# A linear-attention and two-layer expert kernel on one core: the weight slices 5 to 7 are used by the first two token chunks in turn

## The chip, the cores and the metric

One Trainium2 chip; the kernel runs on one of its cores. The engines spoken of are PE (TensorE, matmuls), DVE (VectorE), ACT (ScalarE), POOL (GpSimd) and the queue of SP (SyncE), from which nearly all transfers are issued. The metric is the device time of one execution in microseconds (us); smaller is better.

## What is computed

The reference, cut to what matters. The stages that the change touches are the attention and the first three products of the first expert block (`a`, `b`, `h`).

```python
# attention, per batch (4) and head (8), seq 576, head_dim 64
q_s = softmax(q, axis=-1)                  # over the 64 columns of a row
k_s = softmax(k, axis=2)                   # over the 576 positions
x   = q_s @ (k_s.T @ v)                    # -> 2304 tokens x 512
# first block: w1, w2 512 x 1024, w3 1024 x 1024, w_out 1024 x 512 (given in 8 bytes an element)
a = x @ w1; b = x @ w2
x = (a * b @ w3) @ w_out                   # -> 2304 x 512
# second block: four experts, each relu(x @ e1) @ e2, weighted by domain_probs
```

## The kernel before

Tokens are columns. The 2304 tokens are cut into chunks of 512 (the last one 256); chunk 0 lies in batch 0 (576 tokens a batch), chunk 1 needs the last 64 tokens of batch 0 and 448 of batch 1. The first block's feature dimension is cut into NF = 8 slices f of 128.

**Work per slice.** `ab_step(c, f)` makes `a` and `b` of chunk c for slice f: two accumulations of 12 matmuls of 512 columns (three per 128 rows, since each operand is held as a high and a low part), then a copy of `a` by ACT (L566) and the product with `b` by DVE (L567). With an even f, or any chunk but 0, its two PSUM banks come from `ps_w`, which has two; chunk 0 with odd f takes the banks of `ps_y`. `unit(u)` multiplies a part of w3 with w_out, 12 matmuls; W = w3 @ w_out takes the place of w3 and w_out later.

**Weights come in 8 bytes an element and are converted on the core.** A job is a pair of them: job f is slice f of w1 and w2, job 8 + u is w_out and w3 for unit u, later jobs are two parts of w3. `load_to` issues the transfers (four raw buffers, so job n + 4 waits for job n), `b_to` issues ACT's L140, DVE's four operations L144, L147, L151, L155 and the split into high part (ACT L103) and low part (DVE L104). `convert(n)` issues the loads up to job n + 3 and the conversions up to job n - 1.

**Order.** Work is issued in numbered slots; a scheduler then fixes the order on each engine, early issues first, as far as their inputs are ready by its own estimate. At run time each engine takes its instructions in that fixed order. Slots 6 to 13 (AB0) hold `ab_step(0, 0)` to `ab_step(0, 7)`; slots 14 to 21 (AB1) hold `ab_step(1, 7)` down to `ab_step(1, 0)`, each followed by a unit; slots 22 to 29 (W1) the other eight units; 30 on the product with W. Slices 0 to 5 are written to DRAM during AB0 (`save_w12`) and read again during AB1 (`load_w12`); slices 6 and 7 are kept in SBUF for chunk 1. Weight slices, x, products and W share a pool of 28 tiles.

**Batch 1** must be ready as x before slot 14. `K_SLOT[1]` and `Q_SLOT[1]` give the slots of its four head pairs' keys (6, 7, 8, 9) and its two query halves (6, 8): `k_max`, one slot later `k_exp`, then `k_v` (PE and DVE, ACT), `q_exp`, `q_norm` and `q_turn` (transposes), and `x_stage`, at most in the slot before `X_SLOT[1]`. Loads go three slots earlier. The small PSUM results of these steps share the two banks of `ps_a`. Query half (1, 1) is in `ON_SCALAR`: its exponential is 18 activations of 64 columns with the maximum as bias and a running sum, in place of a subtraction and a sum of the whole tile by DVE. `hold` with `AFTER_JOB` puts an instruction behind the last conversion of a job, but only if that job has been issued by then; with the slots of before this binds batch 1 in one place, `("q", 1, 1): 3` at slot 8.

Of the kernel before, what the change touches and what calls it, by code (L numbers as in the profile page):

```python
# [32 lines left out]
AB0, AB1, W1, Y0, Y1, REST = 6, 14, 22, 30, 38, 46  # L33


PAIRS = [0, 2, 1, 3]
KEPT, SAVE_AT = 2, 2
JOINED = 2
V_WHOLE = (0,)
FILL_T, FILL_B, FILL_V = (5, 3, 3, 12), (0, 3, 3, 0), (0, 0, 0, 0)  # L40
K_SLOT = [[0, 0, 0, 0], [6, 7, 8, 9], [30, 31, 33, 34], [46, 47, 48, 50]]
Q_SLOT = [[2, 2], [6, 8], [30, 32], [46, 48]]
X_SLOT = [AB0, AB1, REST, REST + 8]

AHEAD, AHEAD_ABS = 4, 1

AFTER_JOB = {
    ("k", 1, 0): 2, ("k", 1, 1): 3, ("k", 1, 2): 4, ("k", 1, 3): 5, ("q", 1, 0): 2, ("q", 1, 1): 3,
    ("in", 2): 13, ("q", 2, 1): 16, ("e", 2, 0): 16, ("e", 2, 1): 16, ("k", 2, 2): 16, ("k", 2, 3): 16,
}  # L50

AFTER_Q = {(0, 1): [("q", 1, 0)]}


ON_SCALAR = {(1, 1)}


@with_exitstack
def linear_attention_moe_kernel(ctx: ExitStack, tc, q, k, v, w1, w2, w3, wo, dp, e1, e2, out):
# [4 lines left out]
    NF = w1.shape[1] // 256  # L64
# [21 lines left out]
    def gran(name):  # L86
        return gp.tile([P, 2, 512], F32R, tag="g", name=name)
# [46 lines left out]
    def hold(key, inst):  # L134
        for other in gate.get(key, []):
            after_inst(inst, other)
# [204 lines left out]
    def q_exp(b, j):  # L341
# [3 lines left out]
        hold(("q", b, j), nc.vector.tensor_reduce(out=mx, in_=t, axis=AX.X, op=ALU.max))  # L345
        if (b, j) in ON_SCALAR:
            nc.vector.tensor_scalar(out=mx, in0=mx, scalar1=-1.0, scalar2=None, op0=ALU.mult)
# [22 lines left out]
    def q_norm(b, j):  # L370
        t = qe[b, j].rearrange("p r h d -> p (r h) d")
        n = 2 * QR
        if (b, j) in ON_SCALAR:
            sm = qsm.pop((b, j))
# [55 lines left out]
    before, mid, after = {}, {}, {}  # L430

    def put(d, slot, f, *a):
        d.setdefault(slot, []).append((f, a))

    def run(d, slot):
        for f, a in d.pop(slot, []):
            f(*a)

    for b in range(B):
        for j in range(2):  # L440
            s = Q_SLOT[b][j]
            if b > 0:
                put(before, Q_SLOT[2][j] + 2 if b > 2 else min(s - (3 if b == 1 else 2), Y0 - 1), load_q, b, j)
            put(before, s, q_exp, b, j)
            put(before, s + 1, q_norm, b, j)
            for g in range(3):
                put(after, s + 1, q_turn, b, j, g)
        for i, hp in enumerate(PAIRS):
            s = K_SLOT[b][i]
            if b > 0:  # L450
                put(before, K_SLOT[2][i] + 3 if b > 2 else min(s - 3, Y0 - 1), load_kv, b, hp)
            put(before, s, k_max, b, hp)
            put(before, s + 1, k_exp, b, hp)
            if b < JOINED:
                put(mid, s + 2, k_v, b, hp)
            elif i % 2:
                put(mid, s + 1, k_v2, b, i // 2)
            at = s + (4 if b > 1 else 3)
            if b >= JOINED:
                at = K_SLOT[b][i | 1] + 2 + i % 2 + (b > 1)  # L460
            put(after, min(at, X_SLOT[b] - 1), x_stage, b, hp)

# [10 lines left out]
    w12, w12d = {}, {}  # L473
# [51 lines left out]
    def save_w12(f):  # L525
        for i in range(2):
            w12d[f, i] = dr.tile([P, 2, 512], F32, name=f"w{i}_{f}")
            nc.sync.dma_start(out=w12d[f, i], in_=w12[0, f][i].bitcast(F32))

    def load_w12(c, f):  # L530
        for i in range(2):
            g = gran("wg")
            gate["dma"] = [nc.sync.dma_start(out=g.bitcast(F32), in_=w12d[f, i])]
            if c > 1:
                hold("pace", gate["dma"][0])
            w12.setdefault((c, f), []).append(g)
        if c == NC - 2:
            w12[NC - 1, f] = w12[c, f]
# [70 lines left out]
    def x_free(c):  # L609
        for kk in list(xa.t):  # L610
            if kk[0] == c:
                del xa.t[kk]
# [151 lines left out]
    def slot(s, *steps):  # L764
        run(before, s)
        for f, *args in steps:
            f(*args)
            run(mid, s)
        run(mid, s)
        run(after, s)  # L770
# [21 lines left out]
    def convert(n):  # L792
        load_to(n + AHEAD)
        b_to(n)
# [19 lines left out]

    for f in range(NF):
        convert(f + 2)
        slot(AB0 + f, (ab_step, 0, f))
        if f > 1:
            save_w12(f - 2)
    x_free(0)  # L820
    for f in range(NF - KEPT, NF):
        w12[1, f] = w12[0, f]
    for i in range(NF):
        f = NF - 1 - i
        if f - 2 in range(NF - KEPT):
            load_w12(1, f - 2)
        convert(8 + i + 1)
        slot(AB1 + i, (ab_step, 1, f), *([(unit, i - 1)] if i > 0 else []))
        if 0 <= i - SAVE_AT < KEPT:
            save_w12(NF - 1 - i + SAVE_AT)  # L830
    x_free(1)
    unit(NF - 1)
    steps = [(c, f) for c in range(2) for f in range(NF)]
# [292 lines left out]
    for n in range(NN):  # L1126
# [6 lines left out]
        else:  # L1133
            early, late = mixed.pop(n - 1)
# [45 lines left out]
```

## Time and profile before

| | |
|---|---|
| median of 3 runs | 1142.3 us (1141.69 to 1143.07) |
| profiled execution | 1142.81 us, its span 1141.0 us |
| PE busy | 1120.9 us, 98% of the span |
| DVE busy | 869.1 us, 76% |
| ACT busy | 534.7 us, 47% |
| transfers | 308.04 MB, mean 270 GB/s |

Busy times are of one execution; PE's includes the pipelined tails of matmuls. [...]

### The profile page before, as it was taken

How to read it: one execution, taken by the hardware profiler on the slowest of the kernel's cores; microseconds unless marked ns; L12 is line 12 of the kernel's file. 1: busy time of each engine (PE TensorE's matmuls, PEld its weight loads, DVE VectorE, ACT ScalarE, POOL GpSimd, SP SyncE). 2: the span in 40 equal slices, each digit the busy share in tenths (PEclk: the TensorE clock that was granted, in tenths of full speed). 3: DMA queues.
4: the chain of work that ended last, by engine and by line, in shares of the span. 5: the costliest groups of instructions: out<-in, count | busy, mean ns of one | idle time of the engine just before them, and what ended most of it. 6: DMA issues, size and time to landing. Idle time of an engine off the chain costs nothing.

```text
span 1141.0 us, 18926 instructions
## 1 busy us (share of the span) xinstructions
PE 1120.9 (98%) x7159; PEld 1044.8 (92%) x7159; DVE 869.1 (76%) x1460; ACT 534.7 (47%) x974; POOL 11.4 (1%) x54
## 2 busy tenths in 40 slices
PE   7899999999999999999999999999999999999998
PEld 5677888878888889999999999999999999999998
DVE  7999696856565527999989997777779877777777
ACT  4775245745453326645555444444435434443441
POOL 0000000000010000000000000000000000000000
PEclk8999999999999999999999999999999999999999
DMA  9987962899989768777777888777777797777774
GB/s 266 269 334 289 294 174 83 222 339 396 338 283 396 301 240 311 285 281 272 290 262 289 290 305 289 248 256 251 253 253 249 251 307 249 254 251 250 253 246 128
DMA packets 124667, 308.04 MB, mean 270 GB/s; under 512 B 27936, under 2 KB 51488, under 8 KB 124576
## 3 DMA queue, kind: packets, MB, share of 16 engines
q1 hardware_dynamic: 123616, 306.04, 77.9%
q8 instruction: 57, 0.93, 0.3%
q10 hardware_dynamic: 960, 0.79, 0.3%
q14 instruction: 34, 0.28, 0.1%
HBM read 230.24 MB, written 76.55 MB: 269 GB/s over the span
## 4 chain that ended last, share of the span: by engine, by line
PE 91%; DVE 4%; DMA 3%; SPq 1%; issue 1%; ACT 0%; DVEq 0%; ACTq 0%
PE hp L976 30%; PE op L1053 29%; PE ab L111 5%; PE ab L110 5%; PE ab L109 5%; PE y L110 3%; PE y L111 3%; PE y L109 3%; PE W L109 1%; PE W L110 1%; PE W L111 1%; DMA eg<-e_b 1%; PE xp L405 1%; DMA vt<-in_v_dram 1%; PE kv L294 1%
## 5 line engine op out<-in xcount | busy, mean ns | idle before, releaser
L1053 PE MATMUL op<-eg,h 128*128 128x256 f32 x3024 | 379.8, 280 | 0.8 <-DMA eg<-e_b 0.8
L976 PE MATMUL hp<-t,eg 128*128 128x384 f32 x2016 | 376.9, 336 | 0.9 <-DVE acc L1034 0.9
L1053 PEld LDWEIGHTS op<-eg,h 128*128 128x128 f32 x3024 | 373.5, 188 | 1.2 <-PE hp L976 1.1
L976 PEld LDWEIGHTS hp<-t,eg 128*128 128x128 f32 x2016 | 344.6, 188 | 2.9 <-DVE acc L1034 1.8
L1034 DVE SCALAR_TENSOR_TENSOR acc<-op,prob,acc 128x256 f32<-128x256 f32 (+1 forms) x399 | 197.9, 525 | 42.0 <-PE op L1053 41.9
L103 ACT ACTIVATE h<-blk 128x768 fp32r<-128x768 f32 x168 | 138.0, 843 | 143.1 <-DVE blk L673 108.9
L104 DVE TENSOR_TENSOR h<-blk,h 128x768 fp32r<-128x768 f32 x168 | 157.2, 951 | 24.4 <-ACT h L103 24.3
L959 ACT ACTIVATE blk<-hp 128x384 f32<-128x384 f32 x192 | 90.4, 489 | 141.6 <-PE hp L976 138.1
L963 DVE TENSOR_TENSOR blk<-hp,blk 128x384 f32<-128x384 f32 x144 | 79.3, 556 | 67.0 <-PE hp L976 66.6
L109 PE MATMUL ab<-x,wg 128*128 128x512 f32 (+1 forms) x320 | 120.0, 378 | 1.5 <-ACT bd L308 1.1
L110 PE MATMUL ab<-x,wg 128*128 128x512 f32 (+1 forms) x320 | 118.6, 371 | 1.6 <-ACT x L426 1.4
L111 PE MATMUL ab<-x,wg 128*128 128x512 f32 (+1 forms) x320 | 117.9, 371 | 0.3 <-DVE wg L104 0.3
L965 ACT ACTIVATE blk<-blk 128x768 f32<-128x768 f32 x72 | 60.6, 845 | 73.0 <-DVE blk L963 71.3
L673 DVE TENSOR_TENSOR blk<-blk 128x768 f32<-128x768 f32 x96 | 91.4, 952 | 0.5
L110 PEld LDWEIGHTS ab<-x,wg 128*128 128x128 f32 x320 | 60.3, 189 | 13.1 <-ACT x L426 3.0
L109 PEld LDWEIGHTS ab<-x,wg 128*128 128x128 f32 x320 | 60.1, 189 | 12.7 <-ACT bd L308 1.3
L111 PEld LDWEIGHTS ab<-x,wg 128*128 128x128 f32 x320 | 60.3, 189 | 10.5 <-DVE wg L104 0.7
L567 DVE TENSOR_TENSOR ah<-ab,ah 128x512 f32<-128x512 f32 (+1 forms) x40 | 25.2, 631 | 39.3 <-PE ab L111 39.3
L104 DVE TENSOR_TENSOR eo<-e2r,eo 128x512 fp32r<-128x512 f32 x56 | 37.7, 683 | 20.0 <-ACT eo L103 19.8
L111 PE MATMUL y<-h,W 128*128 128x512 f32 x128 | 50.4, 397 | 0.0
L110 PE MATMUL y<-h,W 128*128 128x512 f32 x128 | 50.4, 394 | 0.0
L109 PE MATMUL y<-h,W 128*128 128x512 f32 x128 | 49.2, 401 | 0.0
(107 smaller groups left out, 1004.2 us busy)
## 6 DMA issues: line engine op xcount, KB each, us to landing
eg<-e_t SPq DMA_DIRECT2D x96, 512.0 KB, 4.5
eg<-e_b SPq DMA_DIRECT2D x72, 512.0 KB, 5.0
eg<-e_s SPq DMA_DIRECT2D x68, 512.0 KB, 4.4
eg<-e_a SPq DMA_DIRECT2D x51, 512.0 KB, 4.6
wg<-w SPq DMA_DIRECT2D x44, 512.0 KB, 8.3
f<-in_moe_w_dram SPq DMA_DIRECT2D x32, 512.0 KB, 6.7
e_t<-eo SPq DMA_DIRECT2D x32, 512.0 KB, 7.5
e_s<-eg SPq DMA_DIRECT2D x28, 512.0 KB, 4.5
```

The lines of the kernel that those rows point to most:

```text
L103: i = nc.scalar.activation(out=hi, in_=src, func=ACTF.Copy)
L104: j = eng.tensor_tensor(out=lo, in0=src, in1=hi.bitcast(F32), op=ALU.subtract)
L109: nc.tensor.matmul(out=ps, lhsT=w_hi, rhs=r_hi, start=first, stop=False, **kw)
L110: nc.tensor.matmul(out=ps, lhsT=w_hi, rhs=r_lo, start=False, stop=False, **kw)
L111: return nc.tensor.matmul(out=ps, lhsT=w_lo, rhs=r_hi, start=False, stop=last, **kw)
L673: return lambda: nc.vector.tensor_tensor(out=dst, in0=x, in1=y, op=op)
L959: nc.scalar.activation(out=block(name)[:, u], in_=src, func=func)
L963: nc.vector.tensor_tensor(out=x[:, u], in0=src, in1=x[:, u], op=ALU.add)
L965: nc.scalar.activation(out=x, in_=x, func=ACTF.Relu)
L976: nc.tensor.matmul(out=q, lhsT=w[:, sw, kt, P * u:P * u + P], rhs=t[b][:, kt, st], start=new and kt == 0 and i == 0, stop=kt == 1 and i == ...
L1034: nc.vector.scalar_tensor_tensor(out=dst, in0=src, scalar=prob[:, T, e:e + 1], in1=dst, op0=ALU.mult, op1=ALU.add,)
L1053: nc.tensor.matmul(out=q[:, c:c + DH], lhsT=g[:, sh, u, P * i:P * i + P], rhs=w[:, sw, u], start=new and u == 0 and j == 0, stop=u == 1 an ...
```

## The change

The slices 5, 6 and 7 (`ALONE = 5` on) are used by chunk 0 and chunk 1 in turn: slots 11, 12 and 13 hold `ab_step(0, f)` and right behind it `ab_step(1, f)`. AB1 then makes slices 0 to 4 of chunk 1, in ascending order, spread over the eight slots in which the units run (slots 14, 15, 16, 18 and 20; the product comes ahead of the unit). Five slices are read again in place of six, each asked for one product ahead; slices 6 and 7 are written to DRAM right after AB0. x of batch 1 must be ready before slot 11: its keys go to slots 4, 4, 5, 5, its queries to 4 and 5, its loads one slot ahead of use, and `q_exp(1, 1)` goes by whole tiles.

```diff
-KEPT, SAVE_AT = 2, 2
+ALONE = 5
-K_SLOT = [[0, 0, 0, 0], [6, 7, 8, 9], [30, 31, 33, 34], [46, 47, 48, 50]]
-Q_SLOT = [[2, 2], [6, 8], [30, 32], [46, 48]]
-X_SLOT = [AB0, AB1, REST, REST + 8]
+K_SLOT = [[0, 0, 0, 0], [4, 4, 5, 5], [30, 31, 33, 34], [46, 47, 48, 50]]
+Q_SLOT = [[2, 2], [4, 5], [30, 32], [46, 48]]
+X_SLOT = [AB0, AB0 + ALONE, REST, REST + 8]
-    ("k", 1, 0): 2, ("k", 1, 1): 3, ("k", 1, 2): 4, ("k", 1, 3): 5, ("q", 1, 0): 2, ("q", 1, 1): 3,
+    ("k", 1, 0): 1, ("k", 1, 1): 2, ("k", 1, 2): 3, ("k", 1, 3): 4, ("q", 1, 0): 1, ("q", 1, 1): 3,
-ON_SCALAR = {(1, 1)}
+ON_SCALAR = set()
-                put(before, Q_SLOT[2][j] + 2 if b > 2 else min(s - (3 if b == 1 else 2), Y0 - 1), load_q, b, j)
+                put(before, Q_SLOT[2][j] + 2 if b > 2 else min(s - (1 if b == 1 else 2), Y0 - 1), load_q, b, j)
-                put(before, K_SLOT[2][i] + 3 if b > 2 else min(s - 3, Y0 - 1), load_kv, b, hp)
+                put(before, K_SLOT[2][i] + 3 if b > 2 else min(s - (1 if b == 1 else 3), Y0 - 1), load_kv, b, hp)
     for f in range(NF):
         convert(f + 2)
-        slot(AB0 + f, (ab_step, 0, f))
+        if f >= ALONE:
+            w12[1, f] = w12[0, f]
+        slot(AB0 + f, (ab_step, 0, f), *([(ab_step, 1, f)] if f >= ALONE else []))
         if f > 1:
             save_w12(f - 2)
     x_free(0)
-    for f in range(NF - KEPT, NF):
-        w12[1, f] = w12[0, f]
+    late = list(range(ALONE))
+    load_w12(1, late[0])
+    for f in range(NF - 2, NF):
+        save_w12(f)
     for i in range(NF):
-        f = NF - 1 - i
-        if f - 2 in range(NF - KEPT):
-            load_w12(1, f - 2)
         convert(8 + i + 1)
-        slot(AB1 + i, (ab_step, 1, f), *([(unit, i - 1)] if i > 0 else []))
-        if 0 <= i - SAVE_AT < KEPT:
-            save_w12(NF - 1 - i + SAVE_AT)
+        steps = [(unit, i - 1)] if i > 0 else []
+        if late and (i % 2 == 0 or len(late) > (NF - i) // 2):
+            steps = [(ab_step, 1, late.pop(0))] + steps
+            if late:
+                load_w12(1, late[0])
+        slot(AB1 + i, *steps)
     x_free(1)
     unit(NF - 1)
```

## Rows read from the trace of the kernel before

**Rows 1.** Stages: start:end, length, busy of PE, PEld, DVE, ACT, POOL, clock, DMA.

```profile
28.00:47.00 19.00, 15.80 (x76) 11.04 (x74) 16.29 (x28) 14.95 (x42) 0.12 (x1) 1.00 1.08 250
47.00:108.80 61.80, 58.51 (x278) 46.66 (x276) 57.20 (x101) 41.91 (x115) 2.02 (x10) 1.00 0.85 303
108.80:165.00 56.20, 56.20 (x250) 46.52 (x249) 46.17 (x64) 20.36 (x34) 0.00 (x0) 1.00 0.91 276
```

**Rows 2.** What PE waited for, 47 to 108.8 us: total, times, longest.

```profile
PE kv L294 <- issue: 1.0, 2, 0.5
PE qt L392 <- ACT qT L394: 0.8, 1, 0.8
PE xp L405 <- DVE x L104: 0.7, 1, 0.7
PE mt L246 <- ACT mx L258: 0.4, 1, 0.4
PE ab L111 <- DVE wg L104: 0.3, 1, 0.3
```

**Rows 3.** PE's products a and b alone, 47 to 108.8 us, with their count.

```profile
47.00:108.80 61.80, 47.43 (x193) 1.00 0.85 303
```

**Rows 4.** PE's timeline: two of these matmuls in an unbroken run, 21 apart.

```profile
103.35 0.39 PE L109 MATMUL ab<-x,wg 128*128 128x512 f32 x1
...
108.11 0.39 PE L109 MATMUL ab<-x,wg 128*128 128x512 f32 x1
```

**Rows 5.** The chain that ended last, 38 to 75 us: start, length, what.

```profile
38.57 7.91 DMA kr<-in_k_dram
...
49.52 0.60 DVE ah L567
50.12 0.60 DVE wg L104
...
53.12 1.21 DVE f L144 x2
...
55.05 0.67 DVE kr L270
55.73 0.60 DVE f L147
...
57.34 2.27 DVE f L151 x2
59.60 1.14 DVE f L155
60.74 1.26 DVE qm L345
...
64.06 0.50 PE ab L111
```

**Rows 6.** ACT by line, 49.2 to 97.2 us: the steps of query half (1, 1).

```profile
L353 ACT ACTIVATE qe<-qr,qm 128x64 f32<-128x64 f32 x18 | 6.0, 337 | 0.0
```

**Rows 7.** ACT's timeline: the exponential of query half (1, 0); what followed (1, 1).

```profile
41.61 1.17 ACT L364 ACTIVATE qe<-qr 128x1152 f32<-128x1152 f32 x1
...
71.76 0.62 ACT L308 ACTIVATE bd<-kv,rs 64x64 f32<-64x64 f32 x2
```

**Rows 8.** DVE's timeline: the one maximum of batch 1's keys that waited for its transfer.

```profile
46.50 0.43 DVE L239 TENSOR_TENSOR m<-kr 128x256 f32<-128x256 f32 x1 [0.67 <-DMA kr<-in_k_dram]
```

**Rows 9.** SP's timeline: job 5's load and the first reload.

```profile
43.67 2.15 SPq L495 DMA_DIRECT2D f<-in_moe_w_dram  x2
...
98.77 2.62 SPq L533 DMA_DIRECT2D wg<-w  x2
```

**Rows 10.** Transfers by line, 0 to 130 us: reloads, KB each, median us to landing.

```profile
wg<-w SPq DMA_DIRECT2D x10, 512.0 KB, 7.3
```

**Rows 11.** PE alone around its last long pause: busy, granted clock, DMA share, GB/s.

```profile
18.00:20.00 2.00, 0.31 (x2) 0.99 1.13 298
20.00:26.00 6.00, 5.90 (x22) 0.50 1.10 341
```

## The prediction

> **What bounds the kernel now.** I read the busy times by stage first. The reader is to see that PE is the bound, and where it is not full: from 108.8 us on PE has no pause at all while the units are made, and there DVE is busy only 46.17 of 56.2 us [rows 1]. No later stage is changed in its work. So whatever the change brings must come out of the stretch in which the slices of chunk 0 are made, 47 to 108.8 us (from the end of the first a and b to the start of the first unit, eight `ab_step` long), and perhaps out of 28 to 47 us, in which batch 0's x is finished. In these PE is busy 58.51 of 61.8 us and 15.8 of 19 us [rows 1]: pauses of 3.3 us and 3.2 us.
>
> Next, what PE waited for in the long stretch. The reader is to see that of the 3.3 us only 0.3 us is a weight slice not yet converted; 2.9 us are hand-overs of batch 1's chain, transposes, `k_v` and `x_stage` behind ACT, DVE or a `ps_a` bank [rows 2]. Third, the chain that ended last: from 46.5 to 64.06 us it runs through DVE alone, through batch 1's keys and queries and the conversion of jobs 3 and 4, and only then through PE [rows 5]. So DVE has a backlog there that PE just lives with; after it, it is ACT and two PSUM banks that hold PE up.
>
> **The prize.** One matmul of `ab_step` costs (108.11 - 103.35) / 21 = 0.227 us [rows 4], so a step of 24 costs 5.44 us and a unit of 12 costs 2.72 us. The 193 of the stretch cost 43.8 us [rows 3]; the other PE work in its busy time, 58.5 - 43.8 = 14.7 us, is batch 1's. The total of PE's work is the same after the change. The pauses, 3.3 us, and some 0.5 us for restarts after five of them are all that can be won there (the latter an estimate: the matmul after a wait shows 0.50 us in the chain where the others take 0.23 [rows 5]).
>
> **The change part by part.**
>
> Order of the products. Counted from 47 us, ahead of the first product of chunk 1 stand now seven steps of chunk 0 (1 to 7), afterwards five (1 to 5). What DVE must have done by then: a slice costs it, by the pieces of the chain, 2 x 0.60 (L144, L147) + 2 x 1.14 (L151, L155) + 2 x 0.60 (the low parts) = 4.7 us, and a product 0.60 us [rows 5]. DVE's 57.2 us of the stretch [rows 1] hold jobs up to 9 and the first three operations of job 10 (2.3 us). Before: up to job 7 is needed, so 57.2 - 2 x 4.7 - 2.3 - 0.6 = 44.9 us, against PE's 58.5 - 5.4 = 53.1 us, 8.2 us to spare. After: up to job 5, so 57.2 - 4 x 4.7 - 2.3 - 3 x 0.6 = 34.3 us, and 2.5 us more for the second query half (below), 36.8 us, against PE's 58.5 - 3 x 5.44 = 42.2 us: 5.4 us to spare. So by count DVE doesn't become the bound, but its margin up to that point shrinks by 2.8 us. From there on it gains: two steps (10.9 us) stand against one slice and two products (5.9 us). I cost the new order at nothing by itself; the cover is these 5.4 us.
>
> Batch 1 earlier. Keys and queries are now issued in slots 4 and 5, ahead of the conversion of job 1 (slot 6), where they stood beside jobs 1 to 5. The gate on `q_exp(1, 1)` behind job 3 falls: at slot 5 only job 0 has been issued, so no entry for batch 1 binds. On DVE, the four passes over half (1, 1) (4 x 1.26 us, the row of L345 being one) and the subtractions of the last two key pairs (0.67 us and a small one each) [rows 5], some 6 to 7 us, can now be placed ahead of jobs 3 and 4. Queued behind them is the low part of job 3, for which PE waited at 64.06 us [rows 5]. PE on its side gets batch 1's 14.7 us to do in the same time. The bounds: 0, if these matmuls fill the gap, and 6.5 us, if none does. I take 0 to 1, since DVE's count above leaves room and PE's work moves with DVE's.
>
> The second query half by whole tiles. Removed from ACT: 18 activations and 18 reads of the sum, one block of 6.0 us that ends at 71.76 us [rows 6, 7]; added one activation of 1.17 us [rows 7]. Added on DVE: a subtraction and a sum over the tile, 2 x 1.26 us, less one small operation, 2.5 us net, beside PE's work, in the margin above. Right behind the block stood `k_v`'s copies to `bd` [rows 7], and the next key exponentials and the copies of the transposes queue behind those; the waits of `qt` and `kv`, 1.8 of the 3.3 us [rows 2], I put down to that jam for the most part. I take half of the stretch's pauses for it, 1.5 us; bounds 0 and 3.3 us.
>
> Loads. The first three requests (queries 0, two key pairs) go out at the same slot 3, behind the loads of jobs 1 to 4; the others move ahead of job 5's load, which now stands before the last keys and sits 2.15 us in issue [rows 9]. So the last keys are asked for some 2 us earlier, and job 5 some 3 us later. DMA is full there, share 1.08 [rows 1], a load of keys took 7.91 us to land [rows 5], and one maximum of keys already kept DVE waiting 0.67 us [rows 8]. Behind such a wait stand the conversions of DVE's queue. Bounds 0 and 2 us, and I take 0: job 5 isn't needed before four more steps, 22 us.
>
> Reloads. Two requests of 512 KB fewer; nothing waits for DMA in that stage, so nothing is won. Slice 0 of chunk 1 is asked for after AB0, as soon as two of the 28 tiles are free; its landing takes 7.3 us [rows 10], and a first request sat 2.62 us in issue [rows 9]. If tiles are free by the end of the last chunk-0 step, the cover is the one step of chunk 1 behind it, 5.4 us; if a step earlier, 10.9 us. Bounds 0 and 4.5 us; I take 0, because six slices were written out before and their tiles are free. The two writes of slices 6 and 7 stand behind that request on SP's queue and delay only the next reload.
>
> Units. Eight units and five products in AB1: PE 8 x 2.72 + 5 x 5.44 = 49.0 us, DVE 8 x 4.7 + 5 x 0.6 = 40.6 us; before 65.3 against 42.4 us. In slots 17, 19 and 21 a unit follows a unit, 2.72 us against 4.7 us of conversion, and with 28 tiles DVE can't run far ahead. DVE had 10 us idle in 108.8 to 165 us [rows 1], so the cover is there; bounds 0 and 3 us (two units that each wait for a split, 1.5 us), taken as 0.
>
> 28 to 47 us. The same matmuls; ACT gets key exponentials of batch 1 between the steps of batch 0's x. Bounds -1 and +1.5 us, taken as 0.
>
> **Sum.** 1142.8 us of the profiled execution - 1.5 = 1141.3 us; that execution stands 0.5 us above the median of the runs (1142.3), so 1140.8 us.
>
> [...]
>
> **Rivals.**
> - *Pauses gone* (faster). Batch 1 is through before the steps in turn, and the stretch runs nearly without a pause: 3.3 us and some of the restarts, 3.5 us: 1138.8 us. For it: DVE's and ACT's margins by count, and the wide cover of 10.9 us from slot 11 on. Against it: the same hand-overs through two `ps_a` banks remain, closer together.
> - *Batch first on DVE* (slower). Place: the low part of job 3, and then job 4. Its price is the 6 to 7 us of batch 1's DVE work placed ahead of them, less what PE has of batch 1 by then; it decides once less than about half of it is ready, because the keys land late [rows 5, 8]. With 3.5 us uncovered: 1145.8 us. A late reload (up to 4.5 us) would give about the same.
> - *Batch first, and the clock falls.* If that pause is as long as the one at 18 us, 6 us at half clock cost another 3 us [rows 11]: 1148.8 us.
> - *It does little.* The gates for batch 1 don't bind, and if the scheduler, which places by its own estimate of readiness, puts batch 1 where it was, time is as before less ACT's part. That lies within the forecast's own range.
>
> **How the numbers follow.** Forecast 0.40, pauses gone 0.38, batch first 0.16, with the clock 0.06. A measurement of this kernel can't tell less than about 0.2%, 2.3 us, from no change: the forecast and its own range, 1140.0 to 1144.6 us, are within it. Faster 0.38, same 0.40, slower 0.22. The range goes from 1137.3 us (pauses gone, and 1.5 us of 28 to 47 us) to 1146.5 us (batch first, with a little more than its price); the clock case and a gain beyond the prize are left out.
>
> **What would show it.** Right: PE's pauses from 47 us to the first unit at 1 to 2.5 us; ACT's L353 gone, no ACT block of 6 us; DVE's L345, L360, L377, L380 of half (1, 1) by about 60 us; no PE wait behind `wg<-w`; after the first product of chunk 1, at about 88 to 92 us, none for DVE either. Wrong upward: PE waits for the low part (L104) of job 3 or 4 for more than 2 us, DVE waits for `kr` or `qr` by transfer, a stretch after 30 us with a clock below 1.0, PE waits in the units from 108.8 us on. Wrong downward: the stretch without pauses, or 28 to 47 us shorter by more than 1 us.

## The result and the profile after

The changed kernel takes 1155.39 us (median of 4 runs, 1153.63 to 1156.40), the kernel before in the same runs 1142.59 us: a ratio of 1.0112 [1.0100, 1.0124], 12.8 us slower. The profiled execution took 1154.75 us, its span 1153.0 us.

The stages of after, in the cuts of [rows 1]: stretch, length, busy time and count of PE, PEld, DVE, ACT and POOL, granted clock (a share of full speed), DMA share, GB/s.

```profile
28.00:47.00 19.00, 16.22 (x74) 11.44 (x73) 17.20 (x28) 14.96 (x43) 0.12 (x1) 0.96 1.10 259
47.00:108.80 61.80, 53.16 (x240) 40.46 (x239) 50.61 (x91) 31.86 (x72) 1.57 (x10) 0.97 0.69 239
108.80:165.00 56.20, 56.20 (x250) 46.53 (x249) 38.03 (x52) 21.23 (x38) 0.00 (x0) 1.00 0.73 245
...
165.00:215.00 50.00, 46.52 (x243) 36.25 (x242) 41.02 (x66) 24.36 (x51) 1.56 (x7) 1.00 0.46 120
```

The last row for the kernel before:

```profile
165.00:215.00 50.00, 50.00 (x260) 40.56 (x260) 34.87 (x57) 30.35 (x62) 1.27 (x10) 1.00 0.49 128
```

The reader is to see three things. PE stands 61.80 - 53.16 = 8.6 us in the long stretch, where it stood 3.3 us. Its clock there is 0.97, which over 61.8 us is another 1.9 us (an estimate from the mean). And it stands 3.5 us from 165 to 215 us, where the kernel before has no pause. That is 5.3 + 1.9 + 3.5 = 10.7 us of the 12.0 us between the spans. DVE, which I feared for, is *less* busy in the long stretch, 50.61 us against 57.20.

PE's products a and b alone, of after: the long stretch (156 matmuls, where [rows 3] has 193), then 60 to 82 us.

```profile
47.00:108.80 61.80, 37.12 (x156) 0.97 0.69 239
...
60.00:82.00 22.00, 0.24 (x1) 0.92 0.41 149
```

The kernel before, the same view, 60 to 82 us:

```profile
60.00:82.00 22.00, 11.77 (x49) 1.00 0.85 315
```

So for 22 us PE gets no a or b, but for one matmul at the very end. What it does there, from PE's timeline of after (start, length; in brackets the idle time before and what ended it):

```profile
59.29 0.40 PE L111 MATMUL ab<-x,wg 128*128 128x512 f32 x1
...
64.17 3.06 PE L294 MATMUL kv<-vt,ek 128*128 128x130 f32 x20 [0.30 <-issue]
69.58 2.07 PE L392 MATMUL qt<-ident,qe 128*128 128x128 f32 x9 [2.36 <-DVE rs L304]
71.57 4.14 PE L294 MATMUL kv<-vt,ek 128*128 128x130 f32 x20
75.64 0.75 PE L405 MATMUL xp<-qT,bd 128*128 128x288 f32 x2
...
81.39 0.75 PE L405 MATMUL xp<-qT,bd 128*128 128x288 f32 x2 [0.99 <-DVE x L104]
81.76 0.61 PE L109 MATMUL ab<-x,wg 128*128 128x512 f32 x1
```

It is batch 1 alone, from its last key maxima over `k_v` to `x_stage`, one short step after another through the two `ps_a` banks. Chunk 0's next slice is converted long before: on DVE's timeline of after, the last conversions of jobs 3 and 4 and, much later, the low part of job 3 are

```profile
60.88 1.20 DVE L155 SCALAR_TENSOR_TENSOR f<-f,f 128x1024 int32<-128x1024 int32 x1
...
64.96 1.21 DVE L155 SCALAR_TENSOR_TENSOR f<-f,f 128x1024 int32<-128x1024 int32 x1
...
74.31 0.16 DVE L301 TENSOR_SCALAR rs<-kv 128x1 f32<-128x1 f32 x1 [4.80 <-PE kv L294]
...
81.69 1.29 DVE L104 TENSOR_TENSOR wg<-f,wg 128x512 fp32r<-128x512 f32 x2 [0.17 <-ACT wg L103]
```

and on ACT's timeline of after the high part of job 3 is made at 81.03 us, 19 us after its conversion ended at 62.08, directly behind x's copies:

```profile
78.44 0.65 ACT L103 ACTIVATE x<-xp 128x128 fp32r<-128x128 f32 x2 [0.39 <-DVE x L104]
...
80.43 0.58 ACT L103 ACTIVATE x<-xp 128x288 fp32r<-128x288 f32 x2 [0.18 <-PE xp L405]
81.03 1.15 ACT L103 ACTIVATE wg<-f 128x512 fp32r<-128x512 f32 x2
```

In those 19 us DVE was busy 10.0 and ACT 10.4 us, mostly with batch 1, so each was idle for some 9 us; the idle 4.80 us before 74.31 stands in the row, and the split of a job takes some 2.4 us (1.15 us on ACT and 1.29 us on DVE in the rows above). What job 3 lacked, as I read it, was not an engine but its turn at the pool of 28: the pool gives its tiles out in the order of issue, and in slot 7 `x_stage` asks for two x tiles of chunk 2 before job 3 and the product (0, 2) ask for theirs, in slot 8 for two more before job 4 does. So the order on ACT has job 3's split behind x's copies. The pool was not used up. Counted from the kernel, job 3's two tiles are the 20th and 21st that are asked for (before them two for the values of batch 0, eight for x of chunks 0 and 1, six for jobs 0 to 2, one for a product, two for x of chunk 2), so it is the order that held them back and not a shortage. Experiment 3 tests this reading. The kernel before shows the same pattern, later and milder; its ACT timeline has, for job 5, converted at 71.41,

```profile
80.34 0.28 ACT L103 ACTIVATE x<-xp 128x128 fp32r<-128x128 f32 x1 [0.39 <-DVE x L104]
80.64 1.15 ACT L103 ACTIVATE wg<-f 128x512 fp32r<-128x512 f32 x2
```

but there PE had two slices in hand.

The clock of after around the pause of 2.36 us (same columns as the stages):

```profile
66.00:68.00 2.00, 1.22 (x10) 0.91 (x8) 1.97 (x7) 1.32 (x5) 0.52 (x3) 1.00 0.66 180
68.00:70.00 2.00, 0.41 (x3) 0.31 (x3) 1.49 (x4) 1.04 (x5) 0.00 (x0) 1.00 0.97 373
70.00:72.00 2.00, 1.87 (x9) 1.29 (x9) 0.00 (x0) 1.47 (x4) 0.00 (x0) 0.62 0.16 64
72.00:74.00 2.00, 2.00 (x10) 1.77 (x9) 0.00 (x0) 0.18 (x1) 0.00 (x0) 0.53 0.00 0
74.00:76.00 2.00, 2.00 (x14) 1.57 (x13) 0.48 (x3) 0.62 (x2) 0.59 (x4) 1.00 0.00 0
```

PE was busy 1.22 and 0.41 of 2 us, then ran at a mean granted clock of 0.62 and 0.53 for some 4 us, near the 0.50 of [rows 11]; the second `k_v` above took 4.14 us where the first took 3.06.

What PE waited for in after (total, times, longest), 47 to 108.8 us, the answer to [rows 2]:

```profile
PE qt L392 <- DVE rs L304: 2.4, 1, 2.4
PE ab L109 <- ACT wg L103: 1.7, 1, 1.7
PE xp L405 <- DVE x L104: 1.7, 3, 1.0
PE mt L246 <- DVE mf L244: 0.6, 1, 0.6
PE xp L405 <- ACT bd L308: 0.6, 1, 0.6
```

and from 108.8 to 215 us, the first two rows (the same question about the kernel before has no row at all):

```profile
PE W L110 <- DVE wg L104: 1.7, 1, 1.7
PE W L109 <- ACT wg L103: 0.9, 1, 0.9
```

### The profile page after: what moved, and what is told of

Same layout as the page of the kernel before. It is cut to its first block, busy times and chain, and to the rows that moved or that the text cites. A ratio compares the mean times of both kernels' runs of the same rounds, so it can differ in the third digit from the quotient of the medians.

```text
span 1153.0 us, 18900 instructions
## 1 busy us (share of the span) xinstructions
PE 1124.3 (98%) x7159; PEld 1044.5 (91%) x7159; DVE 872.0 (76%) x1461; ACT 529.4 (46%) x939; POOL 11.3 (1%) x54
## 4 chain that ended last, share of the span: by engine, by line
PE 85%; DVE 7%; DMA 4%; ACT 1%; issue 1%; SPq 1%; DVEq 0%; ACTq 0%
PE hp L980 29%; PE op L1057 29%; PE ab L109 4%; PE ab L110 4%; PE ab L111 4%; PE y L109 3%; PE y L110 3%; PE y L111 3%; DMA qr<-in_q_dram 1%; DMA eg<-e_b 1%; DMA vt<-in_v_dram 1%; PE xp L405 1%; DMA f<-in_moe_w_dram 1%; DVE f L151 1%; DVE f L155 1%
```

## The experiments

Two theories stood first. **Pool order:** the early `x_stage` takes tiles ahead of job 3 and of chunk 0's products, and so pulls batch 1's serial chain in front of all products. **The rest of the change:** the order in turn, the whole tiles or the reloads cost the time themselves. "Before" is 1141.5 to 1142.6 us in every set of runs, so ratios and differences agree within 1 us.

**1. Batch 1 early and by whole tiles, nothing else of the change** (kernel before with these lines and the loads of the change; order of products, reloads and units as before).

```diff
-K_SLOT = [[0, 0, 0, 0], [6, 7, 8, 9], [30, 31, 33, 34], [46, 47, 48, 50]]
-Q_SLOT = [[2, 2], [6, 8], [30, 32], [46, 48]]
+K_SLOT = [[0, 0, 0, 0], [4, 4, 5, 5], [30, 31, 33, 34], [46, 47, 48, 50]]
+Q_SLOT = [[2, 2], [4, 5], [30, 32], [46, 48]]
-ON_SCALAR = {(1, 1)}
+ON_SCALAR = set()
```

> The kernel before with batch 1 as in the change (keys in slots 4, 4, 5, 5, queries in 4 and 5, loads one slot ahead, second half by whole tiles), but the order of the products a and b, the reloads and the units as before. Theory 1 (the x tiles of batch 1 come ahead of job 3's in the tile pool): the same gap without a product at 60 to 81 us, so 8 to 11 us slower than before, 1150 to 1153 us, and no pause in the units. Rival (the order of the products and the earlier deadline of x make the loss): at most 3 us slower, 1142 to 1146 us.

1154.14 us (1152.34 to 1157.99), ratio 1.0115 [1.0091, 1.0138]: as slow as the whole change. That is 1 us more than the 1150 to 1153 us of the pool theory; the rival's 1142 to 1146 us is out. Its window of 60 to 82 us, all engines, then PE's a and b alone:

```profile
60.00:82.00 22.00, 16.80 (x73) 11.43 (x73) 11.79 (x28) 10.63 (x28) 1.56 (x10) 0.84 0.47 176
...
60.00:82.00 22.00, 0.00 (x0) 0.84 0.47 176
```

The gap and the fallen clock are there; the pauses from 165 us on are not (PE 50.00 of 50 us). So the loss sits in batch 1's new place (with its whole tiles), and the order in turn isn't needed for it.

**2. The same, with `x_stage` back in its slots 9 to 12.**

```diff
-            at = s + (4 if b > 1 else 3)
+            at = s + (4 if b > 1 else 3) if b != 1 else 9 + i
```

> The kernel before with batch 1 early as in the change (slots, loads, whole tiles), but x_stage of its four pairs in slots 9, 10, 11, 12, where it stood before; products, reloads and units as before. Theory 1 (order of the tile pool): the gap at 60 to 81 us came from x_stage's tiles alone, so it is gone: 1142 to 1146 us. Rival (early keys and queries on DVE, ahead of jobs 3 and 4, are the cause): 1149 to 1155 us.

1145.8 us (1144.1 to 1146.84), ratio 1.0035 [1.0021, 1.0048]: 8.3 us come back. PE makes a and b again from 60 to 82 us, at the full clock:

```profile
60.00:82.00 22.00, 11.85 (x48) 1.00 0.83 303
```

**3. The same as 1, with own tiles for chunk 2's x.** `x_stage` stays early; only the pool changes, and the common one has 24 tiles.

```diff
-    NG, NR = 28, 4
+    NG, NR = 24, 4
+    gx = gran_stack.enter_context(tc.tile_pool(name="granx", bufs=4))
-                self.t[key] = gran(f"{self.name}{c}_{kt // per}")
+                self.t[key] = gran(f"{self.name}{c}_{kt // per}") if c != 2 else gx.tile(
+                    [P, 2, 512], F32R, tag="gx", name=f"{self.name}{c}_{kt // per}")
```

> Kernel before with batch 1's keys, queries and loads early and its second query half by whole tiles (as in the run with these alone, 1154.1 us), and with the x tiles of chunk 2 taken from a pool of their own of four tiles (the common pool keeps 24); x_stage stays in its early slots. Theory A (the order in which the one pool gives out its tiles holds job 3's split and chunk 0's products behind batch 1's x): the split no longer waits, PE makes products again from 60 to 82 us (40 or more of its a/b matmuls there, in place of 0), the granted clock stays at 1.0, and some 8 of the 12.3 us come back: 1144.5 to 1147.5 us. Rival B (it is the place of x_stage itself, ahead of the products in the issue order of PE, ACT and DVE, that holds them up; the tiles only come along): nearly no a/b matmul from 60 to 82 us, a clock of 0.8 to 0.9, 1152 to 1155 us.

1144.72 us (1143.08 to 1145.48), ratio 1.0025 [1.0015, 1.0034]: 9.4 us come back without moving a step. PE's a and b alone in this kernel:

```profile
60.00:82.00 22.00, 14.89 (x61) 1.00 1.00 377
```

This tells the pool's order from the place of `x_stage`: with the same slots and the same matmuls, 61 matmuls of a and b in place of none. With its own tiles apart batch 1's x no longer stands before the splits, and the products go ahead of it by themselves; batch 1's first `x_stage` matmul starts at 94.7 us. The total number of tiles is still 28, so it is not more tiles that help.

**4. The same repairs in the changed kernel.** First `x_stage` two slots later (slots 9, 9, 10, 10, the last that the turn at slot 11 allows), then own tiles as in 3.

```diff
-            at = s + (4 if b > 1 else 3)
+            at = s + (4 if b > 1 else 5 if b == 1 else 3)
```

> The changed kernel with x_stage of batch 1 two slots later (slots 9, 9, 10, 10 in place of 7, 7, 8, 8); keys, queries and loads stay as early as in the change. Theory 1 (tile pool order): the splits of jobs 3 and 4 come ahead of batch 1's x, PE makes products during 60 to 81 us, 8 to 10 us come back: 1145 to 1148 us; the pauses in the units at 170 to 195 us remain (2 to 3 us). Theory 2 (DVE backlog): DVE has the same work ahead of jobs 3 and 4, time stays within 2 us of 1155.

> The changed kernel with the four x tiles of chunk 2 in a pool of their own (the common pool has 24 tiles instead of 28, as SBUF has no room for more); all slots as in the change. Theory 1 (tile pool order): no wait of a split behind these tiles at all, so the gap at 60 to 81 us is gone as with x_stage late: 1144 to 1149 us, the upper end if 24 common tiles are too few later. Theory 2 (DVE backlog): 1153 us or more.

1150.22 us, ratio 1.0073 [1.0057, 1.0089], and 1151.53 us, ratio 1.0080 [1.0065, 1.0096]: 5.2 and 3.9 us back, not all. Both lie above what the pool theory gave (1145 to 1148 and 1144 to 1149 us) and below the rival's 1153 us. No run has more than 28 tiles in all, so whether SBUF has room for more isn't shown. The kernel with own tiles, all engines:

```profile
60.00:82.00 22.00, 21.03 (x104) 16.73 (x105) 22.00 (x37) 15.14 (x32) 0.64 (x4) 1.00 0.92 348
82.00:110.00 28.00, 25.33 (x107) 18.87 (x106) 18.70 (x34) 11.66 (x28) 1.39 (x6) 0.94 0.51 188
...
165.00:215.00 50.00, 46.41 (x238) 35.17 (x237) 41.22 (x68) 27.97 (x59) 1.82 (x10) 1.00 0.45 115
```

The stretch from 60 to 82 us is mended; now the chain stands exposed from 82 to 110 us (2.7 us of pauses, clock 0.94), as I read it since chunk 1 wants x at slot 11 whatever the tiles, and the 3.6 us from 165 us on remain. The kernel of 3 has neither: 28.00 of 28 us and 49.99 of 50 us. It has the same pools and the same early batch 1, and differs only in the order of products, reloads and units. So with the pool repaired, the order of three slices in turn, with what it does to reloads and units, costs 1151.5 - 1144.7 = 6.8 us.

**5. The order in turn alone, with slice 7 only** (changed kernel, batch 1's slots, loads and `ON_SCALAR` as before).

```diff
-ALONE = 5
+ALONE = 7
-K_SLOT = [[0, 0, 0, 0], [4, 4, 5, 5], [30, 31, 33, 34], [46, 47, 48, 50]]
+K_SLOT = [[0, 0, 0, 0], [6, 7, 8, 9], [30, 31, 33, 34], [46, 47, 48, 50]]
...
```

> The changed order of products with only slice 7 in turn (ALONE = 7, seven slices read again), and batch 1's slots, loads and second query half as before. Theory 1: no gap at 60 to 81 us, since x_stage stays at slots 9 to 12; what is left is the units' share of the loss: 1144 to 1148 us, with PE pauses in the units. Rival (the order of products costs nothing): 1142 to 1143 us.

1145.7 us (1143.97 to 1148.0), ratio 1.0033 [1.0022, 1.0044]: 3.9 us for something I had costed at nothing. What PE waited for, 100 to 165 us (the profiled execution, 1148.0 us, is the slowest of the seven):

```profile
PE ab L109 <- DVE ah L567: 2.8, 1, 2.8
PE ab L109 <- DMA wg<-w: 0.5, 1, 0.5
```

A product waits once for the product before it to leave its bank, and a reload comes late once; the kernel before has no wait there. Behind the first stands DVE, which makes that product and was late with it. On its timeline:

```profile
155.85 1.35 DVE L345 TENSOR_REDUCE qm<-qr 128x18 f32<-128x1152 f32 x1 [6.64 <-DMA qr<-in_q_dram]
...
159.32 0.68 DVE L567 TENSOR_TENSOR ah<-ab,ah 128x512 f32<-128x512 f32 x1
```

DVE stood 6.64 us for batch 2's queries, with two passes over them and two other operations ahead of the product. The queries were asked for at 141.70 us, where the kernel before asks at 131.92 us. So the 2.8 us are a late transfer seen through DVE's fixed order. This kernel reads seven slices again and the change five, so its 3.9 us are not a part of the change's loss as they stand.

**6. The second query half.** Kernel before with `ON_SCALAR` empty, and changed kernel with `ON_SCALAR` as before.

```diff
-ON_SCALAR = {(1, 1)}
+ON_SCALAR = set()
```

> The kernel before with the second query half of batch 1 by whole tiles (ON_SCALAR empty), nothing else: the second part of the change alone. Theory 1: this part costs and gives little, within 1.5 us of the kernel before. Theory 2: DVE, busy without a break from 46 to 64 us, is 2.5 us later for it, up to 2.5 us slower.

> The changed kernel with query half (1, 1) back on ScalarE (ON_SCALAR as before). Theory 1, order of the tile pool: in the changed kernel the split of job 3 stands behind batch 1's x on ScalarE, because tiles of the common pool are given out in the order of issue and job 3's come behind the x tiles of chunk 2; this edit doesn't touch that, so PE still makes no product a or b from about 60 to 81 us and the time stays at 1153 to 1157 us. Theory 2, DVE's backlog (2.5 us of whole-tile passes plus batch 1 ahead of jobs 3 and 4): the gap shrinks by 2 to 3 us or more, 1151 to 1153 us.

Alone it *costs*: 1144.91 us, ratio 1.0020 [1.0010, 1.0029], 2.3 us by the ratio. That is theory 2's "up to 2.5 us slower", and out of theory 1's 1.5 us. ACT's block is gone and PE waits for DVE in its place, in that kernel from 47 to 110 us:

```profile
PE qt L392 <- DVE qe L380: 2.6, 1, 2.6
```

In the changed kernel taking it back costs too: 1161.12 us, ratio 1.0162 [1.0145, 1.0178], 5.7 us more than the change as a whole, where theory 1 had no difference and theory 2 a gain. There the chain stood bare, and the 18 activations were in it: on ACT they run from 62.88 us to the copy of a transpose out of a `ps_a` bank at 68.85 us and the next key exponential at 69.22 us, and PE goes on with `k_v` at 69.42 us. PE waits there, 47 to 125 us ("issue": the profile names no releaser):

```profile
PE kv L294 <- issue: 5.1, 2, 4.8
```

**7. Own tiles, early batch 1, and 18 activations** (kernel of 3 with `ON_SCALAR` as before), to see whether the last 2.9 us are the whole tiles.

```diff
-ON_SCALAR = set()
+ON_SCALAR = {(1, 1)}
```

> Kernel before with batch 1's keys, queries and loads early and own tiles for chunk 2's x, as in the run that gave 1144.7 us, but the second query half by 18 activations as before. Theory A (the 2.9 us left there are the whole tiles, which alone cost 2.3 to 2.8 us in the kernel before): 1141 to 1143 us, no difference from the kernel before. Rival B (the early slots cost the rest, and in them the 18 activations stand in ACT's way as they did in the changed kernel): 1145 to 1151 us, with a wait of PE behind kv of 3 us or more between 60 and 82 us.

1146.31 us (1146.11 to 1147.48), ratio 1.0031 [1.0018, 1.0044]. Theory A (1141 to 1143 us) falls: nothing comes back. The time lies in B's range. But the wait behind `kv` that B named didn't come either (0.7 us). PE's pauses from 47 to 110 us are 2.6 us here and 3.0 us in kernel 3, no more than before. What the last 3 us of these two kernels are stays open.

**8. Are the pauses of the kernel before waits for tiles?** Kernel before with `x_stage` one slot later, and with own tiles for chunk 2's x.

```diff
-            at = s + (4 if b > 1 else 3)
+            at = s + (4 if b > 1 else 4 if b == 1 else 3)
```

> The kernel before with x_stage of batch 1 one slot later (10 to 13 in place of 9 to 12), nothing else. Theory 1: jobs 5 to 7, which also stand behind x tiles in the kernel before (their splits come 3 to 10 us after their conversion), move ahead of them by one; PE's pauses of 3.3 us between 47 and 108.8 us shrink: 1139 to 1142 us. Rival (those pauses are hand-overs through the two banks of ps_a, whatever the tiles): 1141.5 to 1143.5 us.

> The kernel before with the four x tiles of chunk 2 in a pool of their own (24 common tiles). Theory 1: the splits of jobs 5 to 7 never wait for them, PE's pauses between 47 and 108.8 us shrink by 1 to 3 us: 1139 to 1142 us, if 24 common tiles are enough later. Rival (the pauses are hand-overs of ps_a, and fewer common tiles cost): 1142 to 1147 us.

1143.53 us, ratio 1.0012 [1.0004, 1.0021], and 1142.47 us, ratio 1.0009 [1.0000, 1.0018]: no gain, as the rivals had it, the first at the upper end of its range. In the kernel before the pool's order is covered, as its 0.3 us for a late slice said [rows 2]. That the pauses are hand-overs of `ps_a`, as the rivals say, follows only in so far as tiles are ruled out.

**9. The pauses in the units.** Three attempts on the 3.5 us from 165 us on. Kernel of 4 with later `x_stage`, and own tiles for chunk 1's products (four, the common pool 24); the same kernel with conversions one job further ahead; and the changed kernel with own x tiles and the five late products in the last five slots, the first reload moved along with them (the lines of that, and the pool of the first kernel, are left out below).

```diff
...
-            prods[c, f // 2] = gp.tile([P, 2, 512], F32, tag="g", name="ah")
+            prods[c, f // 2] = (gq if c == 1 else gp).tile([P, 2, 512], F32, tag="g", name="ah")
```
```diff
-        convert(8 + i + 1)
+        convert(8 + i + 2)
-        convert(17 + f // 2)
+        convert(18 + f // 2)
```
```diff
...
-        if late and (i % 2 == 0 or len(late) > (NF - i) // 2):
+        if late and i >= NF - ALONE:
```

> The changed kernel with x_stage two slots later, and the four product tiles of chunk 1 in a pool of their own (24 common tiles). Theory U1: in the second stage the conversions of jobs 11 and on wait in the pool's order behind the product tiles of chunk 1's late slices, DVE idles at 110 to 150 us and lacks the time at 165 to 200 us; with the tiles apart PE's pauses in the units (3.5 to 4 us) go below 1 us: 1146 to 1148 us. Theory U2 (PE makes units faster, 2.72 us each, than DVE converts jobs, 4.7 us, wherever the tiles are): pauses stay, 1149 to 1151 us.

> The changed kernel with x_stage two slots later, and conversions issued one job further ahead in the stages of the units, so that a job's tiles come ahead of the product of the same slot in the pool's order. Theory U1: pauses in the units smaller by half or more, 1147 to 1149 us. Theory U2: unchanged, 1149 to 1151 us.

> Changed kernel with own tiles for chunk 2's x (1151.5 us), and chunk 1's slices 0 to 4 in the last five slots of the units' first half (17 to 21), one each, in place of slots 14, 15, 16, 18 and 20; the first reload goes one slot ahead of use. Theory A (the pauses of 3.6 us between 165 and 215 us come because units stand without products beside them while DVE, which idled earlier with all tiles given out, converts for them): PE is busy over 49 of 50 us there, no new pause over 1 us from 110 to 165 us, 1147 to 1149 us. Rival B (DVE is behind for another reason, the products' place is no matter, or the pause only moves ahead to the slots that now hold a unit alone): PE busy there plus from 110 to 165 us no more than 102 of 105 us, 1150.5 to 1152.5 us.

1151.13 us, ratio 1.0077 [1.0062, 1.0092]; 1149.15 us, 1.0064 [1.0049, 1.0079]; 1150.2 us, 1.0068 [1.0051, 1.0085]. The intervals overlap those of the kernels that they start from (1.0073 and 1.0080). PE's busy time from 165 to 215 us rose from 46.02 us to 48.64 and 48.14 us in the first two, and from 46.41 to 47.19 us in the third: pauses shrank by up to 2.6 us, and the time didn't follow by as much; in the second 1.3 us of them only moved ahead, to 110 to 165 us (53.68 of 55 us busy). So U1, which held that conversions wait for their turn at the pool behind chunk 1's product tiles, has the pauses partly on its side and the time not: the first kernel's time lies at U2's upper end, the second's at the border of the two. In the third, theory A (over 49 us) falls, and time and busy time lie just outside B (1150.5 us, 102 of 105 us).

The pattern that U1 names is on ACT's timeline of after, where ACT stands idle and then makes the high parts of two jobs directly behind the first copy into a new product tile:

```profile
134.04 0.60 ACT L566 ACTIVATE ah<-ab 128x512 f32<-128x512 f32 x1 [7.33 <-PE ab L111]
134.54 2.18 ACT L103 ACTIVATE wg<-f 128x512 fp32r<-128x512 f32 x4
```

What the trace offers beside it is a reading that was not tried apart. SP's queue holds weight loads until a raw buffer is free, and batch 2's loads stand behind them. SP's waits for a raw buffer (total, times, longest), 100 to 180 us, before:

```profile
SPq L495 <- DVE f L155: 15.3, 5, 4.1
```

and after:

```profile
SPq L495 <- DVE f L155: 34.8, 7, 10.0
```

The first queries of batch 2 are asked for at 131.92 us before and at 159.88 us after; their first maximum (L345) comes on DVE at 142.15 and at 167.66 us. In after DVE idles 17.2 of 40 us from 110 to 150 us and is then busy without a break from 170 to 200 us, with batch 2's softmax among the units' conversions. In the kernel before most of that work lay ahead of them. In the first two kernels of this experiment the queries are asked for at 145.79 and 145.04 us, against 154.37 us in the kernel that they start from, and the pauses are smaller; which of the two, pool or queue, is the cause stays open.

**10. Own x tiles, late products, 18 activations** (the third kernel of 9 with `ON_SCALAR` as before), to see whether repairs add up.

```diff
-ON_SCALAR = set()
+ON_SCALAR = {(1, 1)}
```

> As the run with own tiles and late products, and the second query half by 18 activations as in the kernel before. Theory A (the whole tiles saved 5.7 us in the changed kernel only because PE stood at the serial chain; with own tiles the chain is covered and they cost 2 to 3 us as in the kernel before): 2 to 3 us faster than the same kernel with whole tiles, 1144 to 1147 us. Rival B (in the early slots the activations are in the chain's way whatever the pool): 2 to 6 us slower than it, 1149 to 1155 us.

1147.9 us (1147.47 to 1149.31), ratio 1.0046 [1.0031, 1.0061]. It is 2.3 us faster than with whole tiles, as A had it, and 0.9 us above A's range in all. It is the best version found that keeps three slices in turn, and still slower than the kernel before.

## Why the prediction was wrong

**What bounds the kernel** held: PE is the bound, and no version came in below the kernel before. That those pauses are not late weights held too (experiment 8); that they are hand-overs was not tested.

**Batch 1 earlier** is the step that failed. I took 0 to 1 us, "since DVE's count above leaves room and PE's work moves with DVE's", bounds 0 and 6.5 us. Batch 1 early and by whole tiles alone costs 12.3 us (experiment 1), and 9.4 us of that is the order of one pool (3). DVE's count was beside the point: DVE idled. The paragraph follows keys and queries to their new slots and not `x_stage`, which moves with them from slots 9 to 12 to slots 7 and 8, so that half of it is issued ahead of job 3 and all of it ahead of job 4. I had counted engines and queues and left out the tiles, though the text names the pool of 28 for the reloads and the units. The bound was wrong in kind as well: it priced the DVE work that could go ahead of job 3, whereas what went ahead was a serial chain, whose length (22 us) no busy time shows.

**The rival "batch first on DVE"** named the right place, the low part of job 3, and the right order of events. Its engine was wrong, since DVE stood idle for some 9 of the 19 us, and its price of 3.5 us was too small. **The rival with the clock** had the fall right: after the 2.36 us pause the clock fell to 0.62 and 0.53, near the 0.50 of [rows 11]; by the mean clock of 0.97 that cost 1.9 us (an estimate), where I had 3, and its chance was only 0.06. The last section has a longer pause, 2.58 us, at which the clock stayed at 1.00.

**The second query half** was to bring 1.5 us; alone it costs 2.3 us (6). The step that failed is putting the waits of `qt` and `kv` down to ACT's block: without the block `qt` waits 2.6 us for DVE's L380. In the jam of the change it saved 5.7 us, and with own tiles and late products it cost 2.3 us (10): the sign depends on what stands around it, and the runs don't show by what rule.

**Order of the products**, costed at nothing, is a second step that failed: it costs 3.9 us already for one slice (5), and 6.8 us for three once the pool is repaired, units and reloads included (4). The margin of 5.4 us was DVE's by count; the pause of 2.8 us in 5 is DVE standing for batch 2's queries, which no margin of busy time covers. The parts don't add up: 3.9 us for one slice, 12.3 us for batch 1, 12.8 us together. That the order is hidden while PE stands at the chain anyway is likely, and not shown.

**Units** had bounds 0 and 3 us and were taken as 0; the waits for two splits are 2.6 us, the pauses in all 3.5 us. The size of a wait for a split (1.5 us) was right, the value taken was not. "DVE had 10 us idle, so the cover is there" fails as above: DVE idled more, 17.2 us of 40, and earlier than the units wanted it.

**Reloads and loads** held: from 28 to 215 us the profile of after has no wait of PE or DVE for a reload or for batch 1's transfers. **28 to 47 us** held within its bounds: the first product a starts at 32.8 us against 32.3, and the clock of the stretch is 0.96 against 1.00, another 0.8 us (an estimate from the mean).

The sum erred, then, by one term of 12 us, with 3.5 us of units and the sign of the whole tiles beside it. The range failed because the upper bound of that term, 6.5 us, came from the busy time of an engine.

## What to carry to other kernels

Before a stage is moved earlier, list what it *takes* (tiles, banks, raw buffers) and who asks for the same pool next; a pool that is given out in issue order made an unrelated job wait here for the whole chain ahead of it, even with tiles left (job 3's split 19 us in after; tiles apart gave 9.4 us back in experiment 3), and no busy time showed that. In a trace, look for work whose input was long ready and whose engine stood idle: the operation that ended just before it can name the pool. Bound such a move by the length of the chain that comes ahead, not by the busy time of an engine, and give the moved stage's tiles a pool of their own first.

## What the hardware showed unexpectedly

Two cases here show that the length of a pause alone didn't decide whether the clock falls. In after, PE paused 2.36 us, after a stretch in which it was already thinly used (busy 1.22 and 0.41 of 2 us from 66 to 70 us), and ran at 0.62 and 0.53 from 70 to 74 us though it was busy 1.87 and 2.00 of 2 us there. In the kernel before with whole tiles (experiment 6) PE came out of a full stretch, stood 2.58 us, and its clock stayed at 1.00 (what made the difference, the runs don't show): its stretches of 2 us (busy, clock, DMA share, GB/s) are

```profile
72.00:74.00 2.00, 2.00 (x13) 1.00 0.68 279
74.00:76.00 2.00, 1.65 (x8) 1.00 0.02 8
76.00:78.00 2.00, 0.00 (x0) 1.00 0.72 152
78.00:80.00 2.00, 1.52 (x10) 1.00 0.88 358
80.00:82.00 2.00, 1.70 (x8) 1.00 0.85 297
```

The start isn't steady either: the changed kernel and the first kernel of experiment 4 differ from slot 7 on only, yet their profiled executions show a mean clock of 0.78 and 0.88 over the first 28 us, and the first product a at 32.8 and 31.0 us. So these two executions stand 1.8 us apart before the edit begins, and differences of that size are read from medians alone.
